# Decode attention on one core: semaphore waits moved onto the instructions, and another order and cut of the last values

## The chip, the cores and the metric

The kernel runs on one core of a Trainium2 chip. The core has five engines with instruction streams of their own: PE (matrix products; its weight loads are listed as PEld), DVE (vector work), ACT (activations, here exponentials and copies), POOL (here a maximum or sum over partitions) and SP (here it only issues DMAs). They agree with each other through semaphores. Sixteen DMA engines move data between HBM and the core. The metric is the device time of one execution in microseconds; the median of the runs is compared.

## The reference

One query token with 32 query heads attends to 65,536 keys. There are 8 key and value heads, so each serves 4 query heads; a head has 128 elements; all inputs are bf16:

```
B, Hq, Hkv, Sq, Sk, D = 1, 32, 8, 1, 65536, 128
k = jnp.repeat(k, rep, axis=1)          # rep = 4
v = jnp.repeat(v, rep, axis=1)
scores = jnp.einsum("bhqd,bhkd->bhqk", q, k) * D ** -0.5
p = softmax(scores, axis=-1)
out = jnp.einsum("bhqk,bhkd->bhqd", p, v)
```

Keys and values are 134 MB each, and each element is used for 4 query rows only.

## The kernel before

A key/value head is cut into four units (`HU`) of 16,384 keys, so there are 32 units (`NU`). A unit has 128 tiles (`T`) of 128 keys, and its K and its V are one DMA of 4,096 KB each into one of two buffers (`kbuf`, `vbuf`). SP issues all loads in the order K0, K1, V0, K2, V1 and so on; before it reuses a buffer it waits on `kfree` or `vfree`, which ACT and DVE raise when PE has read the buffer. The first and the last K come in halves. The last V comes in six pieces (`V_PIECES`) with a semaphore each (`vpiece`), so that PE can start before all of it is there. Each load is split over the sixteen DMA engines, which raise its semaphore by one each when their share has landed; it counts as landed at sixteen.

PE works through a unit in 16 groups of 8 tiles. A group's key tiles are transposed by PE into a PSUM buffer (`pe_transposes`, four buffers), then copied to SBUF (`ktb`) by DVE or, for every fourth group, by ACT (`evict`), and three groups later PE computes the group's scores (`pe_scores`). DVE takes the maximum of the unit's scores over its tiles, POOL over the partitions, and ACT writes the exponentials (`pts`) with their sums. Then PE multiplies with the values, 128 matmuls into four columns (`pe_values`; `value` is one such matmul). DVE adds the result to the head's running sum `acc` (`add_values`), rescaled as the maximum moves. In the program the values of a unit come after the keys of the next one. PE runs two units in a turn of a hardware loop, DVE and ACT four; DVE's passes -1, 0, 29, 30 and 31 stand outside of the loop, written out one after the other.

Almost all waits go through `take` (lines 33 to 35), which waits for a semaphore and lowers it again. In the profile it is one instruction of its own on the engine, listed under line 35:

```
def take(e, sem, n=1):
    e.wait_ge(sem, n)
    e.sem_inc(sem, -n)
```

The end is `pe_last` on PE with lines 312 to 326 on DVE. The first 120 tiles (`ROWS_FROM`) of the last unit are multiplied as in the other units, with four result columns in `pvb` (line 158), and raise `pvd`; DVE then adds `acc` to the result (line 323) and raises `t_acc`. The last 8 tiles are multiplied the other way round, so that the result lies in rows in `fin` (line 191). Between the fourth and the fifth of these an fp32 matmul with an identity adds the transposed sum `acc` to `fin` (line 190). A small matmul with ones (line 178) gives the sum of the exponentials, and DVE its reciprocal `rl` (line 320, raises `t_last`). DVE scales `fin` with `rl` (line 326), and SP writes the last head's 4 rows (line 410).

## Time and profile before

| what | value |
|---|---|
| median of 3 runs | 633.25 us (633.08 to 633.67) |
| profiled execution | 632.97 us, its span 631.2 us |
| mean granted TensorE clock | 0.772 |
| DMA queue of K and V | 10,232 packets, 268.44 MB, 99.1% of sixteen engines' span |
| PE busy | 520.4 us (82%) |
| DVE busy | 312.4 us (49%) |
| ACT busy | 182.4 us (29%) |
| last issue of a DMA (the output) | 629.59 us from the span's start |

The span runs from the first to the last instruction of the program; the time around it is the rest of the execution. A row of a timeline gives the start and the duration in microseconds, the engine, the line of the kernel, the operation, what it writes and reads, and how many equal instructions were merged into the row; in brackets stand the idle time before it and what ended it. A name with q (PEq, DVEq, SPq) is the engine's sequencer, which waits, branches and issues DMAs. A row of a DMA view gives a queue with its packets, its MB and its share of the sixteen engines; the queues called "instruction" bring in program code.

### The profile page before, as it was taken

To read this page: it belongs to the slowest core of one execution; us is meant where nothing else is said; L and a number is where in the kernel's file an instruction comes from. 1 tells how busy PE (TensorE), PEld (TensorE's weight loads), DVE (VectorE), ACT (ScalarE), POOL (GpSimd) and SP (SyncE) were. 2 spreads that over 40 slices of the span, in tenths; PEclk is the share of its full clock that TensorE was granted. 3 is DMA by queue.
4 is the path that set the end of the run, shared out by engine and by line. 5 is a ranking of instruction groups with operands and counts; after the bars stand their busy time and mean duration, and the time that the engine had idled before them with its cause. 6 is when DMAs were issued, how large, how long until landed. Compare 5 with 4: busy or idle time off the path is not lost. (4 is left out here: it accounts for less than half of the span.)

```text
span 631.2 us, 27735 instructions
## 1 busy us (share of the span) xinstructions
PE 520.4 (82%) x12294; PEld 512.3 (81%) x12294; DVE 312.4 (49%) x689; ACT 182.4 (29%) x410; POOL 15.9 (3%) x49
## 2 busy tenths in 40 slices
PE   4579998879887798878798787988779887879897
PEld 4479997879887788877798787988779877779896
DVE  4445554446544456434565344654445544455552
ACT  2133322123322233221332213332223322133231
POOL 0000000000000000000000000000000000000000
PEclk9788776778776788767887677877678876788776
DMA  8999999999999999999999999999999999999996
GB/s 366 429 432 431 430 430 432 432 432 432 432 432 432 432 432 432 432 432 432 432 432 432 432 432 432 432 432 432 432 432 430 432 432 432 432 432 432 424 437 255
DMA packets 10335, 268.62 MB, mean 426 GB/s; under 512 B 1234, under 2 KB 1490, under 8 KB 1746
## 3 DMA queue, kind: packets, MB, share of 16 engines
q1 hardware_dynamic: 10232, 268.44, 99.1%
q8 instruction: 7, 0.11, 0.1%
q14 instruction: 6, 0.05, 0.0%
q10 hardware_dynamic: 90, 0.02, 0.0%
HBM read 268.44 MB, written 0.01 MB: 425 GB/s over the span
## 5 line engine op out<-in xcount | busy, mean ns | idle before, releaser
L132 PE MATMUL trb<-ident,kbuf 128*128 128x128 bf16 x4096 | 357.1, 246 | 76.1 <-PEq L35 73.3
L132 PEld LDWEIGHTS trb<-ident,kbuf 128*128 128x128 bf16 x4096 | 289.8, 112 | 78.0 <-issue 77.8
L219 DVE COPY ktb<-trb 128x1024 bf16<-128x1024 bf16 x384 | 255.2, 691 | 164.2 <-DVEq L35 163.5
L216 ACT ACTIVATE ktb<-trb 128x1024 bf16<-128x1024 bf16 x128 | 131.0, 1023 | 436.0 <-ACTq L35 436.0
L141 PE MATMUL qkb<-qcur,ktb 128*128 128x4 bf16 x4096 | 173.3, 165 | 22.5 <-PEq L35 20.5
L141 PEld LDWEIGHTS qkb<-qcur,ktb 128*128 128x128 bf16 x4096 | 156.3, 98 | 26.2 <-issue 26.0
L158 PE MATMUL pvb<-pts,vbuf 128*128 128x4 bf16 x4088 | 112.1, 165 | 4.9 <-issue 1.7
L158 PEld LDWEIGHTS pvb<-pts,vbuf 128*128 128x128 bf16 x4088 | 110.0, 101 | 6.8 <-issue 4.3
L339 ACT ACTIVATE pts<-qkb,negm 128x128 bf16<-128x128 f32 x128 | 50.8, 551 | 0.0
L248 DVE TENSOR_REDUCE cmax<-qkb 128x4 f32<-128x512 f32 x32 | 22.1, 692 | 35.2 <-DVEq L35 34.2
L339 ACT ACTIVATION_READ_ACCUMULATOR pts<-qkb,negm 128x1 f32 x128 | 36.1, 282 | 0.0
L237 DVE TENSOR_TENSOR acc<-acc,pvb 128x4 f32<-128x4 f32 x23 | 3.7, 159 | 59.8 <-DVEq L35 59.8
L369 POOL PARTITION_ALL_REDUCE cmaxa<-cmax x32 | 11.9, 370 | 506.3 <-POOLq L35 506.3
L235 DVE COPY acc<-pvb 128x4 f32<-128x4 f32 x8 | 1.3, 162 | 23.8 <-DVEq L35 23.8
L226 DVE COPY qcur<-qT 128x4 bf16<-128x4 bf16 x8 | 1.4, 170 | 10.0 <-DVEq L35 9.9
L278 DVE TENSOR_TENSOR lp<-lp,rsum 128x4 f32<-128x4 f32 x24 | 3.9, 163 | 3.5
L277 DVE TENSOR_TENSOR lp<-lp,alpha 128x4 f32<-128x4 f32 x24 | 3.9, 163 | 3.5
L264 DVE TENSOR_TENSOR dm<-m 128x4 f32<-128x4 f32 x24 | 3.9, 163 | 3.5
L335 ACT ACTIVATE alpha<-dm 128x4 f32<-128x4 f32 x24 | 4.7, 197 | 2.7 <-ACTq L35 2.7
L372 POOL PARTITION_ALL_REDUCE la<-lp x7 | 3.0, 429 | 97.0 <-POOLq L35 97.0
L198 PE MATMUL trb<-ident,qsb 32*128 32x32 bf16 x1 | 0.2, 204 | 5.1 <-DMA qsb<-in_q_dram 5.1
L198 PEld LDWEIGHTS trb<-ident,qsb 32*128 32x128 bf16 x1 | 0.1, 100 | 5.1 <-DMA qsb<-in_q_dram 5.1
(43 smaller groups left out, 32.7 us busy)
## 6 DMA issues: line engine op xcount, KB each, us to landing
vbuf<-in_v_dram SPq DMA_DIRECT2D x31, 4096.0 KB, 31.4
kbuf<-in_k_dram SPq DMA_DIRECT2D x30, 4096.0 KB, 26.8
kbuf<-in_k_dram SPq DMA_DIRECT2D x4, 2048.0 KB, 17.1
vbuf<-in_v_dram SPq DMA_DIRECT2D x1, 2048.0 KB, 17.7
vbuf<-in_v_dram SPq DMA_DIRECT2D x1, 1024.0 KB, 19.8
vbuf<-in_v_dram SPq DMA_DIRECT2D x1, 512.0 KB, 20.3
vbuf<-in_v_dram SPq DMA_DIRECT2D x1, 256.0 KB, 20.5
vbuf<-in_v_dram SPq DMA_DIRECT2D x2, 128.0 KB, 20.2
```

Of the source, the lines that this page charges most:

```text
L132: ins = pe.transpose(trb[j % NTB][:, i * P:(i + 1) * P], kv[:, t, :], ident[:, :])
L141: ins = pe.matmul(qkb[b][:, t * R:(t + 1) * R], lhsT=ktb[:, off:off + P], rhs=qcur[:, :], start=True, stop=True)
L158: return pe.matmul(pvb[b][:, 0:R], lhsT=vv[:, t, :], rhs=pts[b][:, t * R:(t + 1) * R], start=t == first, stop=t == last)
L216: e.activation(dst, trb[j % NTB][:, :], AF.Copy).then_inc(eva, 1)
L219: e.tensor_copy(dst, trb[j % NTB][:, :]).then_inc(evd, 1)
L248: e.tensor_reduce(cmax[:, :], qkb[u % 2][:, :].rearrange("p (t g) -> p g t", g=R), AX.X, ALU.max).then_inc(cm, 1)
L264: e.tensor_tensor(dm[:, :], mo[:, :], mn[:, :], ALU.subtract)
L277: own(e, e.tensor_tensor(lp[:, :], lp[:, :], alpha[:, :], ALU.mult), xd)
L278: own(e, e.tensor_tensor(lp[:, :], lp[:, :], rsum[:, :], ALU.add), xd)
L335: e.activation(alpha[:, :], dm[:, :], AF.Exp, scale=scale)
L339: ins = e.activation(pv[:, g, :], sv[:, g, :], AF.Exp, bias=negm[:, g:g + 1], scale=scale, accum_out=rsum[:, g:g + 1])
L369: e.partition_all_reduce(cmaxa[:, :], cmax[:, :], P, bass.bass_isa.ReduceOp.max).then_inc(cma, 1)
```

## The change

Three things are changed.

First, waits. In `pe_scores` and `evict` the semaphores of the transposes (`trd`, `tra`) and of the copies (`evd`, `eva`) are no longer lowered by one at each group. They count up through a unit, and the k-th group of its kind waits for k; `turn` gives k and whether the group is the last of its kind. The wait is carried by the first matmul of the group or by the copy itself (`wait_op`). Only the last of its kind keeps a separate `take`, which lowers the semaphore by the whole count. In the end the waits on `pvd`, `t_acc`, `s_fin` and `t_last` are written onto the instructions in the same way, and DVE waits for `t_last` ahead of its add.

Second, the cut of the last V: six pieces as before, of 64, 32, 16, 10, 4 and 2 tiles, and the rows form starts with the last piece, at tile 126.

Third, the order at the end: the fp32 matmul of the old sums comes after the last two tiles and ends the accumulation.

```
-V_PIECES = (64, 32, 16, 8, 4, 4)
-ROWS_FROM = 120
+V_PIECES = (64, 32, 16, 10, 4, 2)
+ROWS_FROM = 126
+def turn(j):
+    same = [i for i in range(G) if on_act(i) == on_act(j)]
+    return same.index(j) + 1, j == same[-1]
...
     def pe_scores(pe, b, j):
-        take(pe, eva if on_act(j) else evd)
+        done, (k, last) = eva if on_act(j) else evd, turn(j)
         if j == 0:
             take(pe, qrdy)
+        if last:
+            take(pe, done, k)
         for i in range(TB):
...
+            if i == 0 and not last:
+                ins.wait_op(done, k, "sem-ge")
...
-            if t in starts:
-                pe.wait_ge(vpiece[starts.index(t)], 16)
+            if t == starts[-2]:
+                pe.wait_ge(t_last, 1)
             ins = value(pe, b, t, 0, ROWS_FROM - 1)
+            if t in starts:
+                ins.wait_op(vpiece[starts.index(t)], 16, "sem-ge")
         ins.then_inc(pvd, 1)
-        pe.wait_ge(t_last, 1)
         for t in range(ROWS_FROM, T):
+            ins = pe.matmul(fin[0:R, 0:P], lhsT=pts[b][:, t * R:(t + 1) * R], rhs=vv[:, t, :],
+                            start=t == ROWS_FROM, stop=False)
             if t in starts:
-                pe.wait_ge(vpiece[starts.index(t)], 16)
-            if t == starts[-1]:
-                pe.wait_ge(t_acc, 1)
-                pe.matmul(fin[0:R, 0:P], lhsT=acc[:, :], rhs=identf[:, :], start=False, stop=False)
-            ins = pe.matmul(fin[0:R, 0:P], lhsT=pts[b][:, t * R:(t + 1) * R], rhs=vv[:, t, :],
-                            start=t == ROWS_FROM, stop=t == T - 1)
+                ins.wait_op(vpiece[starts.index(t)], 16, "sem-ge")
+        ins = pe.matmul(fin[0:R, 0:P], lhsT=acc[:, :], rhs=identf[:, :], start=False, stop=True)
+        ins.wait_op(t_acc, 1, "sem-ge")
         ins.then_inc(s_fin, 1)
...
     def evict(e, n, j):
+        k, last = turn(j)
+        if last:
+            take(e, tra if on_act(j) else trd, k)
+        if j == G - 1:
+            e.sem_inc(kfree[n % 2], 1)
         if on_act(j):
-            take(e, tra)
-            if j == G - 1:
-                e.sem_inc(kfree[n % 2], 1)
-            e.activation(dst, trb[j % NTB][:, :], AF.Copy).then_inc(eva, 1)
+            ins = e.activation(dst, trb[j % NTB][:, :], AF.Copy).then_inc(eva, 1)
         else:
-            take(e, trd)
-            e.tensor_copy(dst, trb[j % NTB][:, :]).then_inc(evd, 1)
+            ins = e.tensor_copy(dst, trb[j % NTB][:, :]).then_inc(evd, 1)
+        if not last:
+            ins.wait_op(tra if on_act(j) else trd, k, "sem-ge")
...
-        take(e, pvd)
+        e.wait_ge(t_last, 1)
         b = (NU - 1) % 2
-        e.tensor_tensor(acc[:, :], acc[:, :], pvb[b][:, 0:R], ALU.add).then_inc(t_acc, 1)
-        e.wait_ge(t_last, 1)
-        e.wait_ge(s_fin, 1)
-        e.tensor_scalar(olast[:, :], fin[0:R, 0:P], rl[:, 0:1], None, ALU.mult).then_inc(t_last, 1)
+        ins = e.tensor_tensor(acc[:, :], acc[:, :], pvb[b][:, 0:R], ALU.add)
+        ins.wait_op(pvd, 1, "sem-ge")
+        ins.then_inc(t_acc, 1)
+        ins = e.tensor_scalar(olast[:, :], fin[0:R, 0:P], rl[:, 0:1], None, ALU.mult)
+        ins.wait_op(s_fin, 1, "sem-ge")
+        ins.then_inc(t_last, 1)
...
-        e.wait_ge(t_last, 2)
-        e.dma_start(of[HR - R:HR, :], olast[:, :]).then_inc(o_sem, 16)
+        ins = e.dma_start(of[HR - R:HR, :], olast[:, :])
+        ins.wait_op(t_last, 2, "sem-ge")
+        ins.then_inc(o_sem, 16)
```

More of the change, by code (lines that the diff above doesn't have):

```diff
@@ L179, in pe_last @@
                           start=True, stop=True).then_inc(s_l, 1)
+            if t == starts[-2]:
+                pe.wait_ge(t_last, 1)
+            ins = value(pe, b, t, 0, ROWS_FROM - 1)
             if t in starts:
-                pe.wait_ge(vpiece[starts.index(t)], 16)
-            ins = value(pe, b, t, 0, ROWS_FROM - 1)
+                ins.wait_op(vpiece[starts.index(t)], 16, "sem-ge")
         ins.then_inc(pvd, 1)
-        pe.wait_ge(t_last, 1)
         for t in range(ROWS_FROM, T):
+            ins = pe.matmul(fin[0:R, 0:P], lhsT=pts[b][:, t * R:(t + 1) * R], rhs=vv[:, t, :],
+                            start=t == ROWS_FROM, stop=False)
             if t in starts:
-                pe.wait_ge(vpiece[starts.index(t)], 16)
-            if t == starts[-1]:
-                pe.wait_ge(t_acc, 1)
-                pe.matmul(fin[0:R, 0:P], lhsT=acc[:, :], rhs=identf[:, :], start=False, stop=False)
-            ins = pe.matmul(fin[0:R, 0:P], lhsT=pts[b][:, t * R:(t + 1) * R], rhs=vv[:, t, :],
-                            start=t == ROWS_FROM, stop=t == T - 1)
+                ins.wait_op(vpiece[starts.index(t)], 16, "sem-ge")
+        ins = pe.matmul(fin[0:R, 0:P], lhsT=acc[:, :], rhs=identf[:, :], start=False, stop=True)
+        ins.wait_op(t_acc, 1, "sem-ge")
         ins.then_inc(s_fin, 1)
```

## The prediction

> **What bounds the kernel now.** I read the page first, then its DMA part, the timeline of the last 7 us, and last short stretches around the end.

> ```profile
> span 631.2 us, 27735 instructions
> ...
> vbuf<-in_v_dram SPq DMA_DIRECT2D x31, 4096.0 KB, 31.4
> kbuf<-in_k_dram SPq DMA_DIRECT2D x30, 4096.0 KB, 26.8
> ```

> ```profile
> 15.00:300.00 285.00, 237.48 (x5572) 234.05 (x5570) 141.30 (x300) 82.14 (x182) 6.84 (x18) 0.77 1.00 431
> 300.00:590.00 290.00, 239.97 (x5739) 236.84 (x5736) 143.91 (x315) 84.49 (x191) 7.27 (x19) 0.76 1.00 432
> 626.00:626.41 0.41, 0.36 (x14) 0.28 (x11) 0.00 (x0) 0.00 (x0) 0.00 (x0) 0.50 0.26 86
> 626.41:626.70 0.29, 0.12 (x4) 0.12 (x5) 0.00 (x0) 0.00 (x0) 0.00 (x0) 0.50 0.05 21
> 626.70:627.05 0.35, 0.35 (x16) 0.35 (x15) 0.00 (x0) 0.00 (x0) 0.00 (x0) 0.50 0.07 23
> 627.06:627.40 0.34, 0.27 (x10) 0.18 (x8) 0.00 (x0) 0.00 (x0) 0.00 (x0) 0.50 0.07 24
> 627.41:630.30 2.89, 1.64 (x18) 1.05 (x15) 0.50 (x2) 0.00 (x0) 0.00 (x0) 0.50 0.00 0
> ```

> A row of the second view is a stretch: its length, the busy time of PE, PEld, DVE, ACT and POOL, the granted clock, the DMA share, GB/s. From 15 to 590 us the sixteen DMA engines are full, at 431 to 432 GB/s. 4,096 KB take 9.7 us at that rate but land 26.8 (K) and 31.4 us (V) after their issue: 17 to 21 us of other transfers stand ahead of each. PE, DVE and ACT may be that much early or late and no DMA engine starves. So the time is the bytes, a start, and what stands behind the last byte.

> The end is uneven. From 626.41 to 627.41 the share is 0.05 to 0.07, one engine of sixteen, at 21 to 24 GB/s; the other fifteen are done. That lone engine holds up every piece of the last V, since a piece counts as landed when all sixteen shares are in. After 627.41 nothing is moved; the rest is the tail:

> ```profile
> 627.19 0.05 issue
> 627.24 0.37 PE pvb L158 x8
> ```

> ```profile
> 624.64 0.19 PE L178 MATMUL pvb<-ones,lp 128*4 128x1 f32 x2
> 624.87 0.15 DVE L320 RECIPROCAL rl<-pvb 4x1 f32<-4x1 f32 x1 [0.97 <-PE pvb L178]
> ...
> 627.24 0.29 PEld L158 LDWEIGHTS pvb<-pts,vbuf 128*128 128x128 bf16 x8 [0.16 <-DMA vbuf<-in_v_dram]
> 627.64 0.33 PEld L191 LDWEIGHTS pvb<-vbuf,pts 128*4 128x4 bf16 x4
> 627.67 0.59 PE L191 MATMUL pvb<-vbuf,pts 128*4 128x128 bf16 x4
> 627.76 0.16 DVE L323 TENSOR_TENSOR acc<-acc,pvb 128x4 f32<-128x4 f32 x1 [2.74 <-DVEq L35]
> 628.04 0.14 PEld L190 LDWEIGHTS pvb<-identf,acc 128*4 128x4 f32 x2
> 628.07 0.61 PE L190 MATMUL pvb<-identf,acc 128*4 128x128 f32 x2
> ...
> 628.48 0.63 PE L191 MATMUL pvb<-vbuf,pts 128*4 128x128 bf16 x4
> 629.22 0.34 DVE L326 TENSOR_SCALAR olast<-pvb,rl 4x128 bf16<-4x128 f32 x1 [1.30 <-PE pvb L191]
> 629.59 0.35 SPq L410 DMA_DIRECT2D out_dram<-olast  x1
> ```

> Piece 4 (tiles 112 to 119) has landed at 627.19. The lone engine's eight packets of a 4-tile piece take 0.34 us (the 627.06 row), so pieces 5 and 6 land near 627.53 and 627.87, estimates. Call the last E. The output's DMA is issued at 629.59, E + 1.72.

> The profiled execution took 632.97 us for its span of 631.2; the median of the runs is 633.25, 0.28 more. I work out differences on the profile and take them off the median.

> **Part 1: waits on the instructions, in all passes.**

> ```profile
> L35 DVEq EVENT_SEMAPHORE  x705: 21/21/21, 1.0 to 627.7; - x177
> L35 PEldq EVENT_SEMAPHORE  x671: 51/51/51, 8.2 to 622.4; - x168
> ...
> PE trb L132 <- PEq L35: 73.3, 28, 3.3
> PE qkb L141 <- PEq L35: 20.5, 55, 0.7
> ```

> Line 35 is `take`, one instruction that waits and decrements. Of 16 per pass before score groups 14 go: 448 in 32 passes; before evictions go 11 of 12 on DVE (352) and 3 of 4 on ACT. PE is spared 448 x 51 ns = 23 us, all beside DMA: I take 0 for the end. If the waits cost PE as much instead, 0.7 us per unit, its idle time (73.3 + 20.5 us, 2.9 per unit) and the 17 us of queued DMA cover it. PE's order is unchanged, nothing new is queued behind a wait; SP's and POOL's queues are not touched.

> It also shortens the code, which is read by DMA:

> ```profile
> q8 instruction: 7, 0.11, 0.1%
> q14 instruction: 6, 0.05, 0.0%
> ...
> q14 instruction: 1, 0.01, 1.9%
> ...
> q14 instruction: 1, 0.01, 2.0%
> ...
> q14 instruction: 1, 0.01, 2.0%
> ...
> q1 hardware_dynamic: 658, 12.76, 99.5%
> q14 instruction: 1, 0.01, 0.1%
> ```

> ```profile
> 26.80:83.90 57.10, 28.51 (x60) 0.80 1.01 431
> 83.90:114.10 30.20, 17.90 (x39) 0.77 1.00 430
> ...
> 579.40:601.40 22.00, 10.15 (x21) 0.77 0.99 425
> ```

> The third to fifth lines of the first view are the DMA of 31 to 32, 88 to 89 and 605 to 606 us: one block of code each (about 8 KB: 0.05 MB over 6); the last two are 590 to 620 us. The second counts DVE instructions. DVE enters its loop's fourth pass near 83.9, takes the loop's branch at 114.1 and leaves the last turn at 579.4. Between 26.8 and 83.9 it runs 60 instructions; along the code from 83.9 on, 39 in the loop's rest and 21 behind it until 601.4 make 60 again. Waits and increments included, by the code, both are 128 instructions. Each of these points lies 4 to 5 us before one of the three blocks. So I read them as DVE's: it crosses a block's end at positions 60, 188 and 316 of its code and a block is fetched some 4 to 5 us later, behind queued packets. The third crossing, at 601.4, is in the last pass but one; 70 instructions are left.

> After: 11 fewer in each pass that is written out (passes -1 and 0, four in the loop, 29 and 30), 88, and one fewer net in the end: 89. Then position 316 is 19 past the program's end and the third fetch doesn't come. What it is worth: between 0, if the lone engine is late for another reason, and its whole lag, 1.00 us (626.41 to 627.41). I take 1.00: the lag needs something that hit one engine alone, and the view of 590 to 620 us has one packet outside the queue of K and V, the block of 605 to 606 us. The next engine is late then, at 626.41.

> [...]

> **Part 2: pieces and order at the end.** E' is the new last landing; still six pieces and the same bytes. The 2-tile piece has half the bytes: between 0.17 and 0.34 us on the lone engine, I take 0.19. So piece 4 (10 tiles) lands at E' - 0.53, piece 5 (4) at E' - 0.19.
> - Loads of tiles come (0.29 - 0.10)/7 = 0.027 us apart. Ten from E' - 0.48 and a wait on `t_last` (true since 624.87 + 0.15; about 0.08) put tile 122 at E' - 0.11, after piece 5. Tile 125 loads at E' - 0.03; a group ends 0.18 after its last load began (627.43 to 627.61): `pvd` at E' + 0.15.
> - DVE's add began 0.15 after that behind a separate wait (627.61 to 627.76). With a wait that the instruction carries I have the reciprocal: PE ends 624.83, start 624.87, 0.04. Done at E' + 0.15 + 0.04 + 0.16 = E' + 0.35.
> - Tiles 126 and 127 load from E' + 0.05 and have issued by E' + 0.25: beside DVE's add. If that cover were gone they would cost 0.11 each.
> - fp32 matmul: 0.12 from the add's end to its load before (627.92 to 628.04), 0.04 now; then 0.64 (628.04 to 628.68): E' + 1.03. It no longer has four matmuls behind it (628.68 to 629.11, 0.43).
> - DVE's scaling: 0.04 in place of 0.11, then 0.34; SP 0.03 as before, its wait already rides there: issue at E' + 1.45 for E + 1.72.

> Gain 0.27. If a carried wait saves nothing (0.11 + 0.08 + 0.07 given back) it is 0.01; that is one end, 0.3 the other.

> **Sum.** 1.00 + 0.27 = 1.27: 633.25 - 1.27 = 631.98. With 0.2% (1.27 us, about what a measurement of this kernel can tell from no change) the forecast stands on the line itself.

> **The rivals.**
> 1. *The fetch isn't the cause, or the next late engine is no earlier.* For: the 626.00 row still has 86 GB/s, three or four engines, so engines end unevenly without it too. Against: only one stands a full us apart. Only part 2 counts: 632.98, no change.
> 2. *A full clock in the tail.* Granted clock is 0.50 there and 0.76 on average. At 1.00 PE's share of the new path (0.18 + 0.64 and the loads) is about halved: 0.45 less, 631.53. [...]
> 3. *Slower: PE stalls for code in the tail.* PE's code is 28 instructions shorter per loop, so its block ends move in `pe_last`. Such stalls exist:

> ```profile
> PE trb L132 <- issue: 2.8, 1, 2.8
> PE pvb L158 <- issue: 1.7, 1, 1.7
> ...
> q8 instruction: 1, 0.02, 3.3%
> ```

> The two waits are of the first turn, without a semaphore; the last line is 624 to 626 us, a PE block fetched in the tail. If the moved end needs a block that isn't there: 1.7 to 2.8 on the path, 633.7 to 634.8. It makes the kernel slower by over 0.2% from 1.27 + 1.27 = 2.54 on, so near the upper price, 634.8. Against: the end moves later by 28 instructions, into the same piece, and the block then fetched lies behind the program's end.

> **How the numbers follow.** Forecast 0.60: its size is loose by some 0.5 us (the lag, the carried waits). What I set to 0, 448 waits fewer on PE and the start of the last V's values on PE, can only add to a gain, so I put 0.42 of it at faster and 0.18 at same. Rival 2 0.13, faster. Rival 1 0.16, same. Rival 3 0.11, slower. Faster 0.55, same 0.34, slower 0.11. Range 631.3 to 633.4: from below rival 2 to above rival 1 with the runs' spread (633.08 to 633.67); rival 3 is left out. The forecast's own is 631.5 to 632.5.

> **What would show it.** Code fetches on the 8 KB queue: five in the span, not six, none after 600 us. The stretch with one engine alone: gone or a few tenths. Separate waits at `take`: about 350 on DVE, 220 on PE. fp32 matmul last, output's DMA near 628.3. DMA still 432 GB/s. It is wrong if one engine is still a full us late, if a fetch falls in the last 25 us on a late engine, or if PE idles in `pe_last` without a landing or a sum that it waits for.

## The result and the profile after

The kernel after takes 631.76 us (median of 15 runs, 631.64 to 632.02), the kernel before 633.14 (15 runs, 632.88 to 633.67). The ratio is 0.9978, 95% interval 0.9972 to 0.9985: 1.38 us or 0.22% less, and the runs of the two do not overlap. The forecast was 1.27 us less. The profiled executions took 632.97 us (before) and 631.78 us (after). Two single executions among the experiments below, one of the kernel before and one with five increments, took 719.77 and 718.22 us at a granted clock of 1.00; the ratios leave them out.

The page of the kernel after, its first line, its queues of code, its DMA issues:

```profile
span 629.9 us, 26837 instructions
...
q8 instruction: 7, 0.11, 0.1%
q14 instruction: 6, 0.04, 0.0%
...
vbuf<-in_v_dram SPq DMA_DIRECT2D x31, 4096.0 KB, 31.4
kbuf<-in_k_dram SPq DMA_DIRECT2D x30, 4096.0 KB, 26.9
```

898 instructions fewer are executed, nearly all of them separate waits, and DMA works as before: the transfers land 31.4 us (V) and 26.9 us (K) after their issue, where they landed after 31.4 and 26.8. The row of q14 has the first change in it: 0.04 MB, not 0.05. The DMA of 600 to 625 us shows where the missing block was, first in the kernel after, then in the kernel before:

```profile
q1 hardware_dynamic: 966, 10.47, 99.0%
q8 instruction: 1, 0.02, 0.3%
q10 hardware_dynamic: 12, 0.00, 0.0%
```

```profile
q1 hardware_dynamic: 971, 10.46, 99.0%
q8 instruction: 1, 0.02, 0.3%
q14 instruction: 1, 0.01, 0.1%
q10 hardware_dynamic: 12, 0.00, 0.1%
```

The block of q14 at 605 us is gone. Stretches around the end of the kernel after (length, PE, PEld, DVE, ACT, POOL, clock, DMA share, GB/s):

```profile
626.00:626.40 0.40, 0.29 (x11) 0.20 (x8) 0.00 (x0) 0.00 (x0) 0.00 (x0) 0.50 0.33 95
626.40:626.80 0.40, 0.29 (x10) 0.29 (x11) 0.00 (x0) 0.00 (x0) 0.00 (x0) 0.50 0.03 6
626.80:627.20 0.40, 0.40 (x12) 0.27 (x8) 0.10 (x1) 0.00 (x0) 0.00 (x0) 0.50 0.00 0
```

No engine is alone for 1 us any more; the last bytes move shortly after 626.4, where before they moved until 627.41. The timeline behind them:

```profile
626.51 0.47 PEld L168 LDWEIGHTS pvb<-pts,vbuf 128*128 128x128 bf16 x14 [0.31 <-DMA vbuf<-in_v_dram]
626.51 0.56 PE L168 MATMUL pvb<-pts,vbuf 128*128 128x4 bf16 x14 [0.22 <-DMA vbuf<-in_v_dram]
627.00 0.09 PEld L197 LDWEIGHTS pvb<-vbuf,pts 128*4 128x4 bf16 x2
627.00 0.37 PE L197 MATMUL pvb<-vbuf,pts 128*4 128x128 bf16 x2
627.10 0.16 DVE L336 TENSOR_TENSOR acc<-acc,pvb 128x4 f32<-128x4 f32 x1 [2.99 <-PE pvb L168]
627.32 0.09 PEld L201 LDWEIGHTS pvb<-identf,acc 128*4 128x4 f32 x2 [0.23 <-DVE acc L336]
627.32 0.58 PE L201 MATMUL pvb<-identf,acc 128*4 128x128 f32 x2
627.94 0.34 DVE L339 TENSOR_SCALAR olast<-pvb,rl 4x128 bf16<-4x128 f32 x1 [0.68 <-PE pvb L201]
628.31 0.35 SPq L424 DMA_DIRECT2D out_dram<-olast  x1
```

In the kept traces the last of the sixteen shares of the last piece is counted at 626.95 (E'), against 627.85 in the kernel before (E, estimated at 627.87 in the prediction). The output's DMA is issued at 628.31 (E' + 1.36) instead of 629.59 (E + 1.74). So 0.90 us lie ahead of the last landing and 0.38 behind it.

### The profile page after: what moved, and what is told of

Read it like the earlier page. It is cut to its first block, busy times and chain, and to the rows that moved or that the text cites. A ratio compares the mean times of both kernels' runs of the same rounds, so it can differ in the third digit from the quotient of the medians.

```text
span 629.9 us, 26837 instructions
## 1 busy us (share of the span) xinstructions
PE 517.2 (82%) x12294; PEld 509.2 (81%) x12294; DVE 312.8 (50%) x689; ACT 182.4 (29%) x410; POOL 15.9 (3%) x49
## 5 line engine op out<-in xcount | busy, mean ns | idle before, releaser
L168 PE MATMUL pvb<-pts,vbuf 128*128 128x4 bf16 x4094 | 112.3, 165 | 5.2 <-issue 2.0
L168 PEld LDWEIGHTS pvb<-pts,vbuf 128*128 128x128 bf16 x4094 | 110.2, 101 | 7.2 <-issue 4.6
## 6 DMA issues: line engine op xcount, KB each, us to landing
vbuf<-in_v_dram SPq DMA_DIRECT2D x31, 4096.0 KB, 31.4
kbuf<-in_k_dram SPq DMA_DIRECT2D x30, 4096.0 KB, 26.9
```

The source lines that it names most:

```text
L168: return pe.matmul(pvb[b][:, 0:R], lhsT=vv[:, t, :], rhs=pts[b][:, t * R:(t + 1) * R], start=t == first, stop=t == last)
```

## The experiments

The question is which part earned what, and whether the block of code is the cause of the late DMA engine or only went with it. Theory A is the prediction's: DVE crosses the end of a code block at position 316 of its program, the next block is fetched over a DMA engine that is late already, and that engine ends 1 us later. Theory B is that the order, the cut and the waits of the end earn all. The times in this section are medians of 11 runs, each beside the kernel before on the same chip. The intervals of the ratios are some 0.0009 to each side, that is 0.6 us; but runs of one kernel mostly lie within 0.4 us, and those of the kernels that I set against each other do not overlap where I call them different.

**One part alone: DVE's carried waits.** The kernel before, with this in `evict`:

```
             k, last = turn(j)
             if last:
                 take(e, trd, k)
             ins = e.tensor_copy(dst, trb[j % NTB][:, :]).then_inc(evd, 1)
             if not last:
                 ins.wait_op(trd, k, "sem-ge")
```

> The kernel before; only the 12 evictions per pass on DVE carry their waits (the end, PE and ACT as before). Theory A (code block): DVE's program ends 88 instructions earlier, before position 316; two of its blocks instead of three, no DMA engine alone for 1 us at the end; about 1.0 us less than before, 632.1. Theory B (the gain is in the end's new order and waits, the late engine is late for another reason): as before, 633.1.

Measured: 632.15 us (632.04 to 632.37), ratio 0.9985 (0.9976 to 0.9994). 0.99 us of the gain come with the waits of the evictions on DVE alone, far from the end in the code. The page has 0.04 MB of code on q14, and at the end no engine is alone for 1 us:

```profile
q14 instruction: 5, 0.04, 0.0%
...
626.40:626.80 0.40, 0.40 (x21) 0.40 (x19) 0.00 (x0) 0.00 (x0) 0.00 (x0) 0.50 0.06 17
626.80:627.20 0.40, 0.40 (x13) 0.38 (x11) 0.00 (x0) 0.00 (x0) 0.00 (x0) 0.50 0.00 0
```

Theory B falls. Whether the block or the carried waits themselves pay is not told apart by this run.

**The other part alone: the end.** The kernel after, with `pe_scores` and `evict` of the kernel before:

```
-        k, last = turn(j)
-        if last:
-            take(e, tra if on_act(j) else trd, k)
...
+            take(e, trd)
+            e.tensor_copy(dst, trb[j % NTB][:, :]).then_inc(evd, 1)
```

> The end of the kernel after (cut, order, carried waits there) with the separate waits of the kernel before in all passes. Theory A: position 316 is crossed, the block near 605 us comes and one engine is 1 us late; only the tail is shorter, 0.3 to 0.4 us less than before, 632.8. Theory B: all of the gain, 631.8.

Measured: 632.72 us (632.68 to 633.00), ratio 0.9993 (0.9984 to 1.0002), by the medians 0.42 less than before; the interval takes in no change, and its slowest runs overlap with the fastest of the kernel before (632.90). The medians of the two parts together, 0.99 + 0.42 = 1.41, make up the 1.38. Its stretches at the end have the engine alone again, at 24 to 26 GB/s:

```profile
626.40:626.80 0.40, 0.30 (x12) 0.21 (x8) 0.00 (x0) 0.00 (x0) 0.00 (x0) 0.50 0.07 26
626.80:627.20 0.40, 0.29 (x11) 0.29 (x12) 0.00 (x0) 0.00 (x0) 0.00 (x0) 0.50 0.06 26
627.20:627.60 0.40, 0.30 (x12) 0.21 (x8) 0.00 (x0) 0.00 (x0) 0.00 (x0) 0.50 0.07 24
```

**The length of the code alone.** This tells the block from the waits: the kernel after keeps all its waits and its end, and gets instructions back that do nothing.

```
+    def filler(e):
+        for _ in range(11):
+            e.sem_inc(pad, 1)
...
             for j in part[2]:
                 evict(e, u + 1, j)
+        if has_k(u):
+            filler(e)
```

> The kernel after with 11 increments of an unused semaphore at the end of each DVE pass that has keys: the code is as long as before, no wait or order is changed. Theory A: DVE crosses position 316 again in pass 30, a third block is fetched behind 600 us, one engine is 1 us late: 1.0 us over the kernel after, 632.7 to 632.8. Theory B or any theory in which carried waits gain by themselves: as the kernel after, 631.8.

> As the last, with 27 increments per pass: DVE's code is 216 instructions longer than in the kernel after, 513, and crosses 316 in the loop and 444 in pass 30. Theory A: two more blocks on the same DMA engine, which is 2 us later than in the kernel after: 633.7, and one engine alone for about 2 us at the end. Theory A' (the blocks go to different engines): about as the kernel after, or 1 us over. Theory B: as the kernel after, 631.8, or some tenths more for the 2 us of DVE time per pass.

Measured: 632.69 us (632.61 to 632.99), ratio 0.9994 (0.9985 to 1.0003), with 11 per pass; 633.78 us (633.56 to 633.92), ratio 1.0009 (1.0000 to 1.0018), with 27. So 0.9 us for one block more than in the kernel after and 2.0 us for two. The queue of code of the first, and a stretch at its end with one engine alone:

```profile
q14 instruction: 6, 0.05, 0.0%
...
626.80:627.20 0.40, 0.40 (x16) 0.39 (x15) 0.00 (x0) 0.00 (x0) 0.00 (x0) 0.50 0.06 22
```

The queue of code of the second, and its stretches at the end:

```profile
q14 instruction: 7, 0.06, 0.0%
...
626.80:627.20 0.40, 0.40 (x21) 0.40 (x19) 0.00 (x0) 0.00 (x0) 0.00 (x0) 0.50 0.05 20
627.20:627.60 0.40, 0.34 (x13) 0.25 (x10) 0.00 (x0) 0.00 (x0) 0.00 (x0) 0.50 0.07 26
627.60:628.00 0.40, 0.24 (x9) 0.24 (x9) 0.00 (x0) 0.00 (x0) 0.00 (x0) 0.50 0.06 26
628.00:628.60 0.60, 0.38 (x15) 0.29 (x12) 0.00 (x0) 0.00 (x0) 0.00 (x0) 0.50 0.06 20
```

One engine of sixteen is alone for about 2 us, at 20 to 26 GB/s where it had 21 to 24 alone in the kernel before. The delays add up, as they would if DVE's blocks all went over the same DMA engine.

The packets of the kept traces show that they do. Each of the sixteen engines ends its share of a load with a packet of 4 bytes, sixteen of them for each load, so one can see how far each is behind the first of them. In the kernel before, the latest is 2.09 us behind until the block of 605.5 us and 3.05 behind after it; the next one stays at 2.00. Its block of 88.4 us took one engine from 1.00 to 1.98 behind, the latest from then on, and in the kernel after the block of 109.1 us took one from 1.07 to 2.04. With 27 increments the latest goes from 2.13 to 3.10 at a block of 105.3 us and from 3.38 to 4.35 at one of 614.0 us, while the next one stays at 2.00 and at 2.30. In the kernel after, the latest is 2.05 behind and the next one 1.86. The price of a block can be read there too: it takes 0.32 us itself, and the packet right behind it, the transfer's own 16 KB, takes 1.27 us where those ahead of it take 0.61 to 0.62 (block at 605.5 us of the kernel before; the packet behind took 1.27 in all four profiles with a block at 604 to 606 us). The block and the 0.66 us more of that packet make 0.98 us.

**Where the step lies.** Two and five of these increments per pass, so that the program ends at 313 or 337:

> The kernel after with 2 increments of an unused semaphore per DVE pass that has keys: DVE's program ends at position 313, three short of 316. Theory A (a block is fetched when position 316 is passed): nothing changes, 631.75. Theory D (the later engine of the filler kernels comes from the filler's own work on DVE, in proportion): a fifth of what 11 per pass cost, 631.9.

> The kernel after with 5 increments per DVE pass that has keys: the program ends at 337, so position 316 lies some 21 instructions ahead of its end, in the last pass (about 618 to 621 us). Theory A: the third block comes once more, some 4 us behind, and costs up to 1.0 us as long as its DMA engine still has pieces of V to move: 632.4 to 632.75. Theory D: half of what 11 per pass cost, 632.2, without a block.

Measured: 631.91 us (ratio 0.9982, 0.9973 to 0.9991) with 2 and 632.80 us (ratio 0.9995, 0.9986 to 1.0004) with 5. Between 2 and 5 per pass lie 0.9 us, between 5 and 11 none (632.80 and 632.69): a step, not a slope, and it lies between a program's end at 313 and at 337, as theory A has it for position 316. The DMA of 616 to 624 us with 5 per pass has the block, that of 600 to 625 us with 2 per pass has none on q14:

```profile
q14 instruction: 1, 0.01, 0.3%
```

```profile
q1 hardware_dynamic: 949, 10.43, 98.5%
q8 instruction: 1, 0.02, 0.2%
```

One engine still moves bytes alone from 627.20 to 627.60 there (share 0.06). So even a block that comes this near the last packets, in 616 to 624 us, costs all of it (632.80 against 631.91). The 631.91 of the first is 0.16 more than theory A said and just what theory D said, though its runs (631.78 to 632.52) overlap with those of the kernel after (631.64 to 632.02). The step rules D out, and I have no shown cause for the 0.16. The chain of that profile begins with PE and not with a DMA:

```profile
623.48 0.04 issue
623.52 1.84 PE pvb L170 x64
625.37 0.12 PE pvb L190 x2
625.49 1.87 PE pvb L170 x62
```

There PE came to the last values 1.6 us later than in the kernel after (623.52 against 621.93), and the granted clock of 605 to 610 us was 0.50 where the kernel after had 0.66:

```profile
605.00:610.00 5.00, 5.00 (x73) 5.00 (x71) 2.55 (x7) 0.92 (x2) 0.00 (x0) 0.50 0.99 426
```

```profile
605.00:610.00 5.00, 5.00 (x79) 5.00 (x77) 3.52 (x8) 1.96 (x7) 0.00 (x0) 0.66 1.00 429
```

Its last landing was 0.28 us later too (627.23 against 626.95), without a further block. That is one execution; why the median is higher stays open.

**Another engine's block.** The same filler on ACT instead of DVE:

```
             for j in (7, 11, 15):
                 evict(e, u + 1, j)
+            filler(e)
```

> The kernel after with 11 increments of an unused semaphore at the end of each ACT pass that has keys: ACT's code grows from some 160 to some 250 instructions. Theory A with an engine of its own for each stream's blocks: one more block on the 8 KB queue, but on a DMA engine that isn't the latest: no change against the kernel after, 631.8. Theory A' (any block near the end costs about 1 us): 632.7. If ACT's extra 1 us per pass counts: some tenths over 631.8.

Measured: 631.75 us (631.60 to 631.98), ratio 0.9978 (0.9969 to 0.9988). Its DMA of 600 to 608 us has the extra block, and yet the end is that of the kernel after:

```profile
q14 instruction: 1, 0.01, 0.2%
...
626.00:626.40 0.40, 0.24 (x9) 0.15 (x6) 0.00 (x0) 0.00 (x0) 0.00 (x0) 0.50 0.30 85
626.40:626.80 0.40, 0.34 (x11) 0.34 (x12) 0.00 (x0) 0.00 (x0) 0.00 (x0) 0.50 0.02 4
```

By the packets, the engine that took this block (at 603.8 us) went from 0.98 to 1.65 us behind the first, and the latest one stayed at 2.07. This block, on an engine that was not the last, cost the end nothing (631.75 against 631.76); a block more on the last one cost 0.9 us (11 per pass on DVE, 632.69).

**PE's carried waits.** First the kernel before with them, then the kernel after without them:

```
-        take(pe, eva if on_act(j) else evd)
+        done, (k, last) = eva if on_act(j) else evd, turn(j)
...
+            if i == 0 and not last:
+                ins.wait_op(done, k, "sem-ge")
```

> The kernel before; only PE's score groups carry their waits (448 separate waits fewer on PE). Theory A: PE has slack in every unit and the end is set by DMA: no change, 633.1. Theory C (PE's time counts): up to 23 us of PE time spared, some of it seen: below 632.

> The kernel after with PE's separate waits before the score groups back (448 in all), the rest kept. Theory A as predicted (PE has slack, its carried waits are worth 0 at the end): 631.75. Theory E (with the late DMA engine gone, PE's work on the last two units is nearly the bound; about 1 us later there, it is the bound in some executions, when the clock is granted low): 0.1 to 0.5 us over the kernel after, and in the profile the values of the last V wait for PE's own work or the exponentials, not for landings.

> The kernel after, unchanged, beside the next one on the same chip: 631.75; PE's values of the last piece but three wait for their landing, not for PE.

Measured: 633.10 us against 633.11 of the kernel before (ratio 0.9999, 0.9990 to 1.0008); without them 631.80 us (0.9978, 0.9969 to 0.9987) against 631.73 of the kernel after on the same chip (0.9979, 0.9970 to 0.9988). Both ways nothing that the runs can tell. Theory E had asked for 0.1 to 0.5 us.

**The end taken apart.** The kernel after with separate waits in the end, and with the old pieces (the rows form from tile 124):

```
-        ins.wait_op(pvd, 1, "sem-ge")
+        take(e, pvd)
...
-        ins.wait_op(s_fin, 1, "sem-ge")
+        take(e, s_fin)
```

```
-V_PIECES = (64, 32, 16, 10, 4, 2)
-ROWS_FROM = 126
+V_PIECES = (64, 32, 16, 8, 4, 4)
+ROWS_FROM = 124
```

> The kernel after with separate waits in the end (pvd, t_acc, s_fin as take, the landings as plain waits), cut and order kept. My terms: 0.11 + 0.08 + 0.07 = 0.26 us given back, 632.0. Rival: carried waits save nothing in the end, 631.8.

> The kernel after with the pieces 64, 32, 16, 8, 4, 4 and the rows form from tile 124 (the last piece); order and carried waits kept. My terms: piece 5 lands 0.34 us ahead of the end instead of 0.19, so pvd and the fp32 matmul come some 0.1 us earlier, while four tiles in rows form instead of two have to issue (0.21 more) behind the last landing: within 0.1 us of the kernel after, 631.7 to 631.9. Rival: the cut down to 2 tiles is what pays, 632.1.

Measured: 632.17 us (632.05 to 632.41; ratio 0.9984, 0.9975 to 0.9993) with separate waits, 631.80 us (631.63 to 632.11; ratio 0.9980, 0.9971 to 0.9989) with the old pieces. The timeline of the first:

```profile
626.54 0.64 PE L168 MATMUL pvb<-pts,vbuf 128*128 128x4 bf16 x14 [0.22 <-DMA vbuf<-in_v_dram]
...
627.32 0.16 DVE L337 TENSOR_TENSOR acc<-acc,pvb 128x4 f32<-128x4 f32 x1 [2.66 <-DVEq L41]
627.60 0.12 PEld L202 LDWEIGHTS pvb<-identf,acc 128*4 128x4 f32 x2 [0.40 <-issue]
627.63 0.59 PE L202 MATMUL pvb<-identf,acc 128*4 128x128 f32 x2
628.37 0.34 DVE L340 TENSOR_SCALAR olast<-pvb,rl 4x128 bf16<-4x128 f32 x1 [0.89 <-DVEq L41]
```

From the end of PE's group to DVE's add 0.14 us (627.18 to 627.32) where the carried wait takes 0.03 (627.07 to 627.10), from the add to the fp32 load 0.12 against 0.06, from that matmul's end to the scaling 0.15 against 0.04, and PE's group of 14 takes 0.64 instead of 0.56, where the landing of its last 4 tiles is waited for separately, too: 0.11 + 0.06 + 0.11 + 0.08 = 0.36. By the medians the waits are worth about 0.4 (632.17 against 631.76), about as much as the whole end earns (0.42). With this order the cut down to 2 tiles earns nothing that the runs can tell. The new order has no run of its own.

## Why the prediction was right, point by point

- **DMA bounds it, only the end can pay:** right. All the time is found behind 600 us (the latest DMA engine falls behind at 605.5 us in the kernel before, and the tail is shorter), DMA's rate is unchanged (431 to 432 GB/s from 15 to 590 us), and PE's 448 waits fewer are worth 0 (633.10 against 633.11).
- **The cover of 17 us:** true of the middle only (the upper figure is 31.4 - 9.7 = 21.7, not 21). In the last unit no further transfer stands behind the values, and PE begins them as the landing or the exponentials allow: in the kernel after it had been idle for 0.57 us when the first piece landed (`PE pvb L168 <- DMA` at 621.93), and one execution with a low clock was later by more than that. The step that put PE's cover at the length of the queue was wrong for the end; nothing hung on it here.
- **Position 316 and the third block:** right, by removal (DVE's carried waits alone), by return (11 per pass) and by the step between 313 and 337. The term was 1.00; the medians give 0.99 alone and 0.9 on return. That a block costs the whole lag was taken, not worked out: the price of a block is 0.98 us by the packets, and the lag was 1.05 (3.05 against 2.00).
- **Where a block is paid:** DVE does not wait for the blocks here (in the lists of waits of the two kernels no idle time of DVE is put down to `issue`); the price is paid by the DMA engine that fetches, 0.98 us by the packets and 0.9 to 1.1 us for each block by the medians (0.99, 0.93, 1.09).
- **The tail:** 0.27 by my sum, 0.38 in the profiles, 0.42 alone by the medians. Two terms make most of the difference: the fp32 matmul took 0.58, not 0.64, in the new place, and PE's last group of columns ended at E' + 0.12, not 0.15 (0.02 of that is a slip: by my own terms tile 122 loads at E' - 0.13, not - 0.11). The add came 0.03 behind that group where I had 0.04, the fp32 load 0.06 behind the add where I had 0.04, and the scaling 0.04 behind the matmul, as I had it. Carried waits against separate ones were mis-sized as well: 0.26 by my terms, 0.36 with all of them separate again. There the scaling gave back 0.11 for my 0.07 and the fp32 load 0.06 for my 0.08, and I had left out the 0.08 of the separate wait for a landing within PE's last group.
- **The rivals:** the first (632.98) fell by DVE's carried waits alone and by the fillers. The second didn't come, the clock at the end is 0.50 again. Its 0.45 us was an estimate that took all of PE's part as halved at a clock of 1.00: in the kernel before, eight transposes took 1.01 us at 0.50 (608.43) and 0.61 at 1.00 (610.24), but eight matmuls into four columns 0.40 and 0.34. The third didn't either: q8 has its 7 blocks and PE waits for landings in the last pieces.
- **Code blocks in the span:** I said five on the 8 KB queue, and the page says 6 packets and 0.04 MB; five blocks of 8 KB are 0.04 MB, so the sixth is a small packet, not a block (40 bytes at 0.05 us; the same kernel's second profile has five packets). The separate waits left are 352 on DVE and 223 on PE, and the output's DMA is issued at 628.31, as the prediction's signs had it.

## What to carry to other kernels

In a kernel that DMA bounds, look at the last microseconds by stretches: here a share of 0.05 to 0.07, one engine of sixteen, for 1.00 us meant that one DMA engine was late, and the question was what else that engine had carried. It had carried the blocks of DVE's program, though DVE was busy for only 49% of the span: three instructions fewer per pass (2 instead of 5 increments) kept the program short of the next block and the time 0.9 us lower. What such a block less is worth here ends where the next engine is the last: in the kernel after that one is 0.19 us ahead of the latest, so a further block less would be worth about 0.2 us, an estimate from 2.05 and 1.86. At the very end of a kernel, where engines hand over one to another, waits carried by the instructions were worth 0.06 to 0.11 us each here.
